# A decode kernel: TensorE's program shortened with loops, output turns moved ahead of w2, and hints on the last branches

## The chip, the cores and the metric

The kernel runs on one core of one Trainium2 chip. The metric is the device time of one execution in microseconds (us). Most numbers below are medians of five or six executions; the profile of a kernel is one execution with the profiler on. Kernels are compared only within the same rounds.

## The reference

It is one decoding step of a transformer block for 8 sequences: attention over a cache of 4096 keys, and an MLP beside it, both on the normalized input.

```python
# B, D = 8, 576; H, Sk, Dh = 32, 4096, 128; F = 4608; all bfloat16
x  = A_x
xn = _layernorm(x)
q  = (xn @ wq)                       # 8 x 32 heads x 128
p  = softmax(q . k_cache * Dh**-0.5) # k_cache, v_cache: 8 x 32 x 4096 x 128
o  = (p . v_cache) @ wo
y  = _layernorm(xn)
h  = gelu(y @ w1 + b1)
return x + o + (h @ w2 + b2)
```

The two caches are 537 MB. Everything else that is loaded (wq, w1, w2, wo) is 20 MB.

## The kernel before

The work is cut into 32 tiles of (sequence, 8 heads). K and V of a tile are 8.4 MB each and go through a ring of nearly three tiles in SBUF. SyncE issues all big DMAs in one order: wq, w1, K0, V0, K1, V1, ..., K31, V31, w2, wo. A tile's K is multiplied by the query on VectorE, summed on TensorE (with identity weights) and VectorE; V is multiplied on TensorE.

Before the first tile there is a head: layernorms, `turn_both` (small operands transposed on TensorE), `queries`, their broadcast, and the MLP's first layer with its gelu. V0 may not be loaded before the head's attention part is done, K1 not before the MLP part is done and the first two products of tile 0, V1 not before tile 0 has used V0:

```python
    def turn_both(e):
        for c in range(WC):                      # 9 matmuls
            i = e.matmul(tp[:, c], lhsT=dupv[:, c, :], rhs=two, start=True, stop=True)
        return i
    # ... cut ...
    def queries(e):
        for c in range(WC):                      # 36 matmuls, each into one of 4 groups of 32 columns
            wv = wq_sb[:, c, :].rearrange("p (x m d) -> p m x d", m=M, d=Dh)
            for m in range(M):
                i = e.matmul(
                    S_ps[0][m * MP:(m + 1) * MP, :], lhsT=xT[:, c, :], rhs=wv[:, m],
                    start=(c == 0), stop=(c == WC - 1))
        return i
    # ... cut ...
    for token in (wq_read, *head_done):
        od.wait("sync", token)
    load_kv(v_v, 0, 1)
    for token in mlp_done:
        od.wait("sync", token)
    for t in range(1, NT):
        sy.wait_ge(sem["kf"], NX * (t - 1) + 2)
        load_kv(k_v, t, 0)
        sy.wait_ge(sem["vf"], t)
        load_kv(v_v, t, 1)
```

After the last tile comes the tail: w2 (72 matmuls in two halves), the turning of the attention outputs (8 small matmuls) between the halves, and wo (64 matmuls in four pieces as they land):

```python
    CUTS = (0, 12, 23, 30, RO)                   # wo in pieces of 12, 11, 7, 2 rows; RO = 32
    # ... cut ...
    te.wait_ge(w2_in, 16)
    hidden_part()                                # 36 matmuls
    te.wait_ge(sem["on"], NT)
    ot = S_ps[0][:, :RO * B].rearrange("p (r b) -> p r b", b=B)
    for b in range(B):
        ins = te.matmul(
            ot[:, :, b], lhsT=Ox[:, b * NHG:(b + 1) * NHG].rearrange("p n g m -> p (n g m)"),
            rhs=low[:], start=True, stop=True)
    ins.then_inc(sem["end"], 1)
    hidden_part()                                # 36 matmuls
    te.wait_ge(sem["on"], NT + 1)
    for n, (r0, r1) in enumerate(zip(CUTS, CUTS[1:])):
        te.wait_ge(wo_in[n], 16)
        # ... two matmuls a row ...
    ins.then_inc(sem["end"], 1)
```

The softmax here doesn't subtract the row's maximum and nothing guards it: scores larger than these inputs give would overflow.

## Time and profile before

| | |
|---|---|
| time, first three executions | 1292.75 us (1292.69 to 1292.96) |
| span of the profiled execution (first to last instruction) | 1291.5 us |
| DMA rate over the span | 431 GB/s |
| busy: TensorE, VectorE | 57 %, 64 % |
| from one K or V tile's landing to the next | 19.35 us |

Parts of the page of the kernel before: the head line, and one line of the span in 40 equal slices. `DMA` is the busy share of the 16 DMA engines in tenths.

```profile
span 1291.5 us, 14658 instructions
...
DMA  9999999999999999999999999999999999999998
```

The DMA line is full up to the last slice. The view of waits says the same from the other side. Its columns are the waiting engine, its tile and line, whom it waited for, the total in us, how often, and the longest.

```profile
DVE ring L559 <- DMA ring<-in_A_k_cache_dram: 281.3, 31, 9.1
...
SPq L271 <- PE tot_ps L666: 634.8, 31, 20.7
SPq L271 <- PE s_ps L643: 525.7, 30, 17.6
```

VectorE waits up to 9 us in each tile for K, while SyncE waits for buffers with its queue still full. So the stream of DMA is the limit, and only three things can move the time: a gap in the stream, the last landing, and what comes after it. Two stretches must therefore be read closely. First, SyncE's issues in the head (start, duration, what):

```profile
1.26 0.33 SPq L271 DMA_DIRECT2D ring<-in_A_k_cache_dram  x1
23.95 0.33 SPq L271 DMA_DIRECT2D ring<-in_A_v_cache_dram  x1
53.53 0.33 SPq L271 DMA_DIRECT2D ring<-in_A_k_cache_dram  x1
74.24 0.33 SPq L271 DMA_DIRECT2D ring<-in_A_v_cache_dram  x1
92.05 0.33 SPq L271 DMA_DIRECT2D ring<-in_A_k_cache_dram  x1
```

These are K0, V0, K1, V1, K2. Each transfer lands in 16 parts; the first part of K1 lands at 83.28 us and the last at 85.16, so V1, issued at 74.24, is in the queue some 9 us before the stream needs it. That is the slack of the head. Second, the tail, from the timeline of the kernel before:

```profile
1277.94 3.67 PE L374 MATMUL acc<-ring,hT_sb 128*8 128x288 bf16 x36 [2.77 <-DMA ring<-in_B_w_dram]
...
1281.55 0.41 PE L692 MATMUL s_ps<-low,Ox 128*128 128x32 bf16 x8
...
1281.88 2.37 PE L374 MATMUL acc<-ring,hT_sb 128*8 128x288 bf16 x36
...
1284.09 3.29 PE L374 MATMUL acc<-ring,OT 128*8 128x288 bf16 x46
...
1288.31 1.27 PE L374 MATMUL acc<-ring,OT 128*8 128x288 bf16 x18 [0.92 <-DMA ring<-in_A_wo_dram]
...
1289.62 0.45 DVE L604 CAST fin<-acc 8x288 bf16<-8x288 f32 x1 [7.20 <-PE acc L374]
```

The bracket is the idle time before the group and what ended it. TensorE waits for w2 (2.77 us), works through it, and waits again for wo. The first 36 matmuls of w2 took 0.10 us each (3.67 / 36), the second 36 took 0.066: the granted clock was 0.50 of full speed from 1277.2 to 1280.6 us and 1.0 after it. The end of the chain of waits confirms who is last:

```profile
1259.74 28.52 DMA ring<-in_A_wo_dram
1288.26 0.04 issue
1288.31 1.29 PE acc L374 x18
1289.60 0.02 issue
1289.62 0.45 DVE fin L604
```

The third wo piece landed at 1288.26 and the fourth at 1288.96 (the landings in the trace).

### The profile page before, as it was taken

What the parts mean: (1) busy time and instruction counts of PE and PEld (TensorE: products, weight loads), DVE (VectorE), ACT (ScalarE), POOL (GpSimd) and SP (SyncE); (2) the same over time, 40 slices, a digit from 0 to 9 for tenths busy, and PEclk for the clock granted to TensorE, in tenths of its full rate; (3) what the DMA queues carried; (4) which work ended last, traced back from release to release, by engine and by line L of the source; (5) the groups of instructions that cost most, each with busy time, mean ns of one, the idle gap of its engine ahead of it and who ended that gap; (6) DMA issues with size and microseconds to landing.
All of it is one profiled execution on the core that took longest, in us unless ns stands there. A gap on an engine that the chain in (4) does not pass through costs nothing. (4 is left out here: it accounts for less than half of the span.)

```text
span 1291.5 us, 14658 instructions
## 1 busy us (share of the span) xinstructions
PE 736.8 (57%) x4707; PEld 322.3 (25%) x4707; DVE 829.4 (64%) x740; ACT 56.8 (4%) x181; POOL 2.4 (0%) x12
## 2 busy tenths in 40 slices
PE   4654565554565554665554565554566554565557
PEld 1222232222222222222222232222222222222223
DVE  2655677655677655677655677655677655577654
ACT  2000000000000000000000000000000000000000
POOL 0000000000000000000000000000000000000000
PEclk8778887778887777887777887778887777888779
DMA  9999999999999999999999999999999999999998
GB/s 419 441 427 440 430 428 449 422 428 449 422 428 449 422 430 447 422 436 440 424 436 438 426 438 434 428 442 428 428 449 422 428 449 422 428 449 422 430 447 350
DMA packets 10410, 557.02 MB, mean 431 GB/s; under 512 B 1163, under 2 KB 1188, under 8 KB 1446
## 3 DMA queue, kind: packets, MB, share of 16 engines
q1 hardware_dynamic: 10368, 556.93, 99.7%
q8 instruction: 3, 0.05, 0.0%
q10 hardware_dynamic: 38, 0.02, 0.0%
q14 instruction: 1, 0.01, 0.0%
HBM read 556.94 MB, written 0.01 MB: 431 GB/s over the span
## 5 line engine op out<-in xcount | busy, mean ns | idle before, releaser
L643 PE MATMUL s_ps<-ring,ident 128*128 x2048 | 544.5, 423 | 514.1 <-PEq L641 513.1
L559 DVE TENSOR_TENSOR ring<-ring,qb 128x4096 bf16<-128x4096 bf16 x256 | 579.2, 2283 | 281.6 <-DMA ring<-in_A_k_cache_dram 281.3
L643 PEld LDWEIGHTS s_ps<-ring,ident 128*128 128x128 bf16 x2048 | 217.4, 106 | 828.3 <-issue 678.5
L534 DVE TENSOR_REDUCE sc<-s_ps 128x32 f32<-128x512 f32 x256 | 171.8, 684 | 0.0
L662 PE MATMUL o_ps<-ring,ebd 128*32 128x512 bf16 x2048 | 116.4, 380 | 0.0
L546 DVE TENSOR_TENSOR ebd<-es,head 128x1536 bf16<-128x1536 bf16 x64 | 77.9, 1218 | 0.0
L569 DVE RECIPROCAL rec<-tot_ps 128x8 f32<-128x8 f32 x32 | 6.6, 208 | 110.7 <-PE oT_ps L670 110.7
L582 ACT ACTIVATE es<-sc 128x192 bf16<-128x192 f32 x64 | 19.8, 310 | 1104.2 <-DVE sc L534 1104.2
L662 PEld LDWEIGHTS o_ps<-ring,ebd 128*32 128x32 bf16 x2048 | 51.6, 97 | 62.5 <-issue 13.6
L670 PE MATMUL oT_ps<-selc,ob 128*128 128x8 f32 x256 | 33.9, 259 | 12.3 <-ACT ob L586 12.3
L670 PEld LDWEIGHTS oT_ps<-selc,ob 128*128 128x128 f32 x256 | 31.0, 191 | 15.2 <-ACT ob L586 15.2
L586 ACT ACTIVATE ob<-o_ps 128x512 f32<-128x512 f32 x32 | 19.1, 597 | 80.2 <-PE o_ps L662 80.2
L425 DVE TENSOR_SCALAR ring<-ring 96x384 f32<-96x384 f32 x2 | 0.7, 352 | 26.4 <-ACT ring L424 26.4
L545 DVE TENSOR_TENSOR Es<-Ep 128x1 f32<-128x1 f32 x32 | 5.1, 160 | 13.3 <-ACT es L582 13.3
L666 PEld LDWEIGHTS tot_ps<-headf,Es 128*128 128x128 f32 x64 | 9.5, 187 | 13.6 <-issue 13.6
L666 PE MATMUL tot_ps<-headf,Es 128*128 128x8 f32 x64 | 12.4, 266 | 0.0
L582 ACT ACTIVATION_READ_ACCUMULATOR es<-sc 128x1 f32 x64 | 11.9, 186 | 0.0
L414 PE MATMUL o_ps<-ring 128*32 128x384 bf16 x27 | 7.8, 860 | 2.8 <-DMA ring<-in_B_w_dram 2.8
L574 DVE TENSOR_TENSOR Ox<-on,quad 128x32 bf16 x32 | 6.2, 192 | 4.8
L414 PE MATMUL s_ps<-ring 128*32 128x384 bf16 x27 | 7.9, 862 | 0.0
L374 PE MATMUL acc<-ring,hT_sb 128*8 128x288 bf16 x72 | 6.0, 335 | 2.8 <-DMA ring<-in_B_w_dram 2.8
L336 PE MATMUL tot_ps<-ident,ring 40*128 40x16 bf16 x9 | 0.7, 204 | 11.8 <-DVE ring L314 11.8
(76 smaller groups left out, 61.2 us busy)
## 6 DMA issues: line engine op xcount, KB each, us to landing
ring<-in_B_w_dram SPq DMA_DIRECT2D x2, 5184.0 KB, 25.2
ring<-in_A_wq_dram SPq DMA_DIRECT2D x1, 4608.0 KB, 13.7
ring<-in_A_wo_dram SPq DMA_DIRECT2D x1, 1728.0 KB, 28.6
ring<-in_A_wo_dram SPq DMA_DIRECT2D x1, 1584.0 KB, 26.5
ring<-in_A_wo_dram SPq DMA_DIRECT2D x1, 1008.0 KB, 28.5
ring<-in_A_k_cache_dram SPq DMA_DIRECT2D x32, 31.9
ring<-in_A_v_cache_dram SPq DMA_DIRECT2D x32, 30.5
ring<-in_A_wo_dram SPq DMA_DIRECT2D x1, 288.0 KB, 28.8
```

Of the source, the lines that this page charges most:

```text
L414: i = e.matmul(h_ps[j][s * MP:(s + 1) * MP], lhsT=lhsT, rhs=wv[:, r0:r0 + HK, :], **flags)
L534: ins = ve.tensor_reduce(out=sc[:, n * CB:(n + 1) * CB], in_=bank_of(x).rearrange("p (c d) -> p c d", d=DL), axis=AX.X, op=ALU.add)
L546: ve.tensor_tensor(out=ebd[:, ja:jb], in0=es[:, a:b].rearrange("p (j c) -> p j c", c=4).unsqueeze(2) .to_broadcast([P, nj, G, 4]), in1=hea ...
L559: ve.tensor_tensor(out=k, in0=k, in1=qb[:, bass.ds(t, 1), :].to_broadcast([P, CB, Dh]), op=ALU.mult,).then_inc(sem["prod"], 1)
L569: ve.reciprocal(out=rec[:], in_=tot_ps[:, :G]).then_inc(sem["rec"], 1)
L574: ve.tensor_tensor(out=Ox[:, bass.ds(t, 1)].rearrange("p o g m -> p (o g) m"), in0=on[:].unsqueeze(2).to_broadcast([P, G, M]), in1=quad[:] ...
L582: sa.activation(out=es[:, a * CB:b * CB], in_=sc[:, a * CB:b * CB], func=ACT.Exp, scale=scale, accum_out=Ep[:, i:i + 1]).then_inc(sem["x"], 1)
L586: sa.activation(out=ob[:].rearrange("r c d -> r (c d)"), in_=o_ps, func=ACT.Copy).then_inc(sem["ob"], 1)
L643: ins = te.matmul(to, lhsT=idn, rhs=k[:, :, d * DL:(d + 1) * DL], start=(d == 0), stop=(d == Dh // DL - 1))
L662: ins = te.matmul(o_ps[m * MP:(m + 1) * MP, :], lhsT=ebd[:, j].rearrange("p g c -> p (g c)"), rhs=vals[:, c:c + 4, :], start=(j < M), stop ...
L666: te.matmul(tot_ps[:, :G], lhsT=Es[:].to_broadcast([P, P]), rhs=headf[:], start=True, stop=True).then_inc(sem["vf"], 1)
L670: ins = te.matmul(oT_ps[:, :G], lhsT=ob[:, c, :], rhs=selc[:, c, :], start=(c == 0), stop=(c == 3))
```

## The change

Its intent, as far as the diff shows it: a shorter TensorE program (about 705 instructions instead of about 790, as the prediction counts them), so that fewer blocks of instructions have to be fetched; small operands' turns and the queries become loops; the MLP layer works in groups of 512 columns; the output turns go ahead of w2, into TensorE's wait for it; and the last branch of VectorE and of TensorE gets a branch hint. Two small moves (a drain at the start, a buffer in the head) are left out below. The core of the diff:

```diff
+    def looped(name, n, **steps):
+        regs = {k: nc.alloc_registers(f"{name}_{k}", engines=[ENG.PE]) for k in steps}
+        # ... registers set, jump to a block of its own; close() adds the steps and branches back ...
     def turn_both(e):
-        for c in range(WC):
-            i = e.matmul(tp[:, c], lhsT=dupv[:, c, :], rhs=two, start=True, stop=True)
-        return i
+        (c, at), close = looped("turn_both", WC, c=(0, 1), at=(0, 2 * B))
+        e.matmul(
+            tot_ps[:, bass.ds(at, 2 * B)], lhsT=dupv[:, bass.ds(c, 2 * D - WC + 1)][:, ::WC],
+            rhs=two, start=True, stop=True)
+        close()
+        return nothing(e, oT_ps[:1, :1], idn[:, :1], idn, True)
     def queries(e):
-        for c in range(WC):
-            ... four matmuls, each into its own 32 columns ...
+        def part(at, w, start):
+            wv = ring[:, bass.ds(w, HQ)].rearrange("p (x m d) -> p m x d", m=M, d=Dh)
             for m in range(M):
+                e.matmul(
+                    S_ps[0], lhsT=xTz[:, bass.ds(at + (M - 1 - m) * MP, P)], rhs=wv[:, m],
+                    start=start and m == 0, stop=False)
+        part(0, 0, True)
+        (at, w), close = looped("queries", WC - 1, at=(M * MP, M * MP), w=(HQ, HQ))
+        part(at, w, False)
+        close()
+        return nothing(e, S_ps[0][:, :1], idn, xTz)
@@ layer @@
-        for j in range(HJ):
-            for s in range(HS):
-                ... 2 x 3 matmuls of 384 columns ...
+        for j, s, r0, r1 in HG:      # 4 matmuls of 512 columns, 1 of 256
+            i = e.matmul(h_ps[j][s * MP:(s + 1) * MP], lhsT=lhsT, rhs=wv[:, r0:r1, :], **flags)
@@ tail @@
+    vector_last = nc.mark_branch_hint_location(ENG.DVE)      # at VectorE's start
+    ve.br("vector_end").branch_hint(vector_last)             # at its end
+    place = nc.mark_branch_hint_location(ENG.PE)             # after the last tile
+    te.wait_ge(sem["on"], NT)
+    heads = Ox[:].rearrange("p t g m -> p (t g m)")
+    (b, at), close = looped("turn_out", B, b=(0, 1), at=(0, P))
+    te.matmul(
+        S_ps[0][:, bass.ds(b, RO * B - B + 1)][:, ::B], lhsT=heads[:, bass.ds(at, P)], rhs=low[:],
+        start=True, stop=True)
+    close()
+    nothing(te, S_ps[1][:1, :1], idn[:, :1], idn, True).then_inc(sem["end"], 1)
     te.wait_ge(w2_in, 16)
     hidden_part()
-    te.wait_ge(sem["on"], NT)
-    ... the 8 output turns, written out ...
     hidden_part()
     # ... wo as before ...
+    te.br("tensor_end").branch_hint(place)
```

(`nothing` is a matmul of one column whose end is signalled; a loop has no last matmul that could carry the signal.)

## The prediction

> **What bounds it now.** The DMA stream. The page's slices show DMA at 9 tenths or more in all but the last slice, 431 GB/s mean. Each 8.4 MB K or V tile lands 19.35 us after the one before (trace landings). The engines wait: the view of waits has VectorE 281 us on K tiles, the SP queue over 1100 us on buffers. So only what delays the stream, the last landing, or the work after it, can move the time. The chain of waits ends: last wo pieces landed 1288.26 and 1288.96 us, 18 matmuls (1.27 us), VectorE copy 0.45 us, output DMA 1.4 us.

> **What changes.**
> 1. Fewer TensorE instructions (about 790 to 705, from the build): of the three TensorE fetches (29.9, 76.0, 1287.1 us) I expect one, near 50 us. The VectorE hint should suppress the one at 52 us. The tail depends on the latest engine, so going from three late engines to one gains only 0.1 to 0.2 us. None late would gain 1.3 us.
> 2. Head: the looped turn costs about 0.5 us a pass (register ops 0.12 each, compare-branch 0.27, read off the product loop): 9 passes, 4.5 us for 0.7. Queries lose the four concurrent column groups (36 matmuls of 512 columns in 4.0 us): alone 0.427 us each at the cold clock, half warm: about 10 us, ending near 27 us instead of 17.9. Layer: same column total, about 13.7 us. VectorE's first tile starts at 52 to 54 us instead of 46.8. It is absorbed: V1 is issued at 74.2 us while K1 streams until 83, so 7 to 9 us are free.
> 3. Tail: the eight output turns (0.41 us) become a loop of about 4 us from 1276, ahead of w2, which landed at 1277.9. The w2 part then starts near 1280, with more of it at the 0.5 clock (0.102 us a matmul cold, 0.066 warm). Before, TensorE waited about 1.3 us for wo; that is used up: matmuls end near 1290.3 instead of 1289.6. This costs 0 to 1.5 us.
> [...]

> Sum: -0.15 + 0.8 - 0.2, about +0.4 us.

> **Predicted: 1293.1 us, range 1291.3 to 1294.8.** Faster by over 2%: 0.005; within 2%: 0.97; slower by over 2%: 0.025.

> **Signs.** Right: landings still 19.35 us apart; TensorE fetch packets 3 to 1; queries 10 us; V1 issued before 83 us; no TensorE wait on wo in the tail. Wrong: a gap in the DMA slices before 100 us; all three late DMA engines gone and the last landing near 1287.6 (then near 1291.5 us); an out-turn loop much under 4 us.

> **What would make it wrong by much.** The build puts a block boundary inside the TensorE product loop, run 256 times. [...] VectorE's loop of before seems to span a boundary with a single fetch, so I give this little chance.

Its sum came to about +0.4 us with all its terms; the -0.2 in it is the term of the end hints, worked out from no measurement. Without that term the sum is +0.65. A block is, here and below, what one fetch packet of 16384 bytes brings; where blocks end in the program is the author's reading of the build.

## The result and the profile after

| | before | after |
|---|---|---|
| time, six executions each | 1292.82 us (1292.69 to 1293.05) | 1294.51 us (1294.10 to 1295.43) |
| span of the profiled execution | 1291.5 us | 1293.4 us |
| its time less its span (unrounded, 1291.52 and 1293.38) | 1.36 us | 1.36 us |
| last wo landing | 1288.96 us | 1289.11 us |
| VectorE's copy of the result starts | 1289.62 us | 1291.47 us |
| last output transfer is issued | 1290.09 us | 1291.94 us |

The ratio is 1.0014, with a 95 % interval of 1.0001 to 1.0027. A ratio here is the mean time of one kernel's fast runs over that of the other's in the same rounds, so not quite the ratio of the medians above. Within 2 % it is the same; it is slower by 1.7 us all the same, and none of the six runs overlaps a run of before. The profiled executions differ by 1.86 us in time and by 1.85 us in the start of the final copy. So all of the loss arises before that copy, and nothing is gained or lost behind it.

The same two lines of the kernel after. The DMA line is as full as it was, up to the last slice:

```profile
span 1293.4 us, 14753 instructions
...
DMA  9999999999999999999999999999999999999997
```

SyncE's issues in the head, K0 to K2:

```profile
1.26 0.33 SPq L288 DMA_DIRECT2D ring<-in_A_k_cache_dram  x1
33.48 0.33 SPq L288 DMA_DIRECT2D ring<-in_A_v_cache_dram  x1
59.76 0.33 SPq L288 DMA_DIRECT2D ring<-in_A_k_cache_dram  x1
80.46 0.33 SPq L288 DMA_DIRECT2D ring<-in_A_v_cache_dram  x1
91.52 0.33 SPq L288 DMA_DIRECT2D ring<-in_A_k_cache_dram  x1
```

V0 is 9.5 us later, K1 and V1 6.2 us, K2 not at all. V1, at 80.46 us, is still ahead of K1's first landing (83.16). The cause is in the head's groups of the kernel after (busy us, mean ns of one, then idle before and why):

```profile
L409 PE MATMUL s_ps<-ring 128*128 (+1 forms) x36 | 10.7, 473 | 0.5 <-DVE ring L384 0.5
L375 PE MATMUL tot_ps<-ident,ring 40*128 40x16 bf16 x9 | 2.0, 221 | 14.5 <-DVE ring L331 12.0 <-issue 2.5
```

The same group of queries took 4.0 us before (36 matmuls of 512 columns), four column groups side by side; now a matmul starts 0.427 us after the one before it until 22.6 us. The nine turns now last from 11.99 to 16.46 us in the timeline; before they took 0.70 us. K1 lands at 85.01 us (85.16 before), V1 at 104.36 (104.51): the later head left no gap.

The tail of the kernel after, from its timeline (the first and last pass of the loop are shown):

```profile
1276.16 0.23 PE L738 MATMUL s_ps<-low,Ox 128*128 128x32 bf16 x1 [1.14 <-DVE Ox L619]
...
1280.00 0.23 PE L738 MATMUL s_ps<-low,Ox 128*128 128x32 bf16 x1 [0.29 <-issue]
...
1280.26 7.24 PE L421 MATMUL acc<-ring,hT_sb 128*8 128x288 bf16 x72
...
1287.33 4.09 PE L421 MATMUL acc<-ring,OT 128*8 128x288 bf16 x64
1291.47 0.45 DVE L649 CAST fin<-acc 8x288 bf16<-8x288 f32 x1 [10.58 <-PE acc L421]
```

No TensorE group after the loop has an idle time in brackets: TensorE no longer waits for wo at all. The end of the chain of waits, in which DMA no longer appears:

```profile
1280.00 0.23 PE s_ps L738
1280.24 0.02 issue
1280.26 0.16 PE s_ps L366
1280.42 11.02 PE acc L421 x135
1291.44 0.02 issue
1291.47 0.45 DVE fin L649
```

The 1.85 us can be added up from the two timelines. The w2 matmuls start 2.32 us later (1277.94 to 1280.26). From their start to the first wo matmul it is 6.15 us before, with the turns in the middle, and 7.07 us after, without them: 0.92 more. From there to the copy it is 5.53 us before, with the waits for wo, and 4.14 after, without: 1.39 less. 2.32 + 0.92 - 1.39 = 1.85. The middle term depends on where the half clock ended in these two executions.

The loop goes round every 0.53 us, of which a matmul shows 0.23 busy. And the clock is still down when w2 starts. In stretches of the kernel after, from 1276.00 to 1280.40 and from there to the end of w2 (busy time of each engine and instruction counts, then granted clock, DMA share, GB/s):

```profile
1276.00:1280.40 4.40, 2.01 (x11) 0.96 (x13) 0.00 (x0) 0.00 (x0) 0.00 (x0) 0.50 1.01 427
1280.40:1287.30 6.90, 6.90 (x73) 4.31 (x70) 0.42 (x1) 0.00 (x0) 0.00 (x0) 0.61 0.94 391
```

The clock's own records put the half clock from 1275.49 to 1285.73 us, three stretches of 3.413 us, against one such stretch (1277.22 to 1280.64) before. So 5.5 us of the w2 part ran at half clock, against 2.7 before. That is not the loop's doing alone: in head_last_hint below, without the loop, TensorE waits idle for w2 and 6.0 us of the w2 part run at half clock. In both records every stretch of either clock is 3.413 us or a multiple of it (up to seven times), but for the last, which the end of the record cuts short. What decides between the two clocks the records do not say, and TensorE's busy time as profiled gives no sharp limit: at half clock, a stretch of 3.41 us with 2.70 busy (24 matmuls, 1277.22 to 1280.64) was followed by the full clock in the kernel before, and one with 2.76 busy (22 matmuls, 1278.90 to 1282.32) by more half clock in the changed kernel.

### The profile page after: what moved, and what is told of

The parts are those of the page before. It is cut to its first block, busy times and chain, and to the rows that moved or that the text cites. A ratio compares the mean times of both kernels' runs of the same rounds, so it can differ in the third digit from the quotient of the medians.

```text
span 1293.4 us, 14753 instructions
## 1 busy us (share of the span) xinstructions
PE 739.4 (57%) x4700; PEld 325.1 (25%) x4700; DVE 829.5 (64%) x740; ACT 56.5 (4%) x181; POOL 3.2 (0%) x12
## 5 line engine op out<-in xcount | busy, mean ns | idle before, releaser
L690 PE MATMUL s_ps<-ring,ident 128*128 x2048 | 537.1, 418 | 514.9 <-PEq L688 514.9
L460 PE MATMUL o_ps<-ring 128*32 128x512 bf16 (+1 forms) x40 | 12.8, 1079 | 0.0
L627 ACT ACTIVATION_READ_ACCUMULATOR es<-sc 128x1 f32 x64 | 11.9, 186 | 0.0
L409 PE MATMUL s_ps<-ring 128*128 (+1 forms) x36 | 10.7, 473 | 0.5 <-DVE ring L384 0.5
```

The source lines that it names most:

```text
L409: e.matmul(S_ps[0], lhsT=xTz[:, bass.ds(at + (M - 1 - m) * MP, P)], rhs=wv[:, m], start=start and m == 0, stop=False)
L460: i = e.matmul(h_ps[j][s * MP:(s + 1) * MP], lhsT=lhsT, rhs=wv[:, r0:r1, :], **flags)
L627: sa.activation(out=es[:, a * CB:b * CB], in_=sc[:, a * CB:b * CB], func=ACT.Exp, scale=scale, accum_out=Ep[:, i:i + 1]).then_inc(sem["x"], 1)
L690: ins = te.matmul(to, lhsT=idn, rhs=k[:, :, d * DL:(d + 1) * DL], start=(d == 0), stop=(d == Dh // DL - 1))
```

## The experiments

Two theories were tested. The *loop theory*: the loss is TensorE's tail, that is the loop's 4 us in front of w2 and the half clock at which w2 then runs. The *fetch theory*: the loss is on the DMA side, from instruction fetches among the last transfers (the after trace has one at 1284.0 us), and from the head. A further question is what the fetches do to the stream at all. "Before" beside each run is the kernel before in the same rounds.

| run | time us (range) | before in the same rounds |
|---|---|---|
| turn_flat | 1293.19 (1292.77 to 1293.38) | 1292.92 (1292.81 to 1293.41) |
| before_turn_loop | 1294.18 (1293.83 to 1294.61) | the same |
| no_hints | 1294.17 (1293.94 to 1294.95) | the same |
| turn_loop_warm | 1293.12 (1292.86 to 1294.10) | the same |
| tail_of_before | 1292.92 (1292.90 to 1293.49) | 1292.88 (1292.68 to 1293.23) |
| head_last_hint (one look) | 1292.88 | the same |
| head_last_pad (one look) | 1293.08 | the same |
| before_cuts | 1293.04 (1292.93 to 1293.18) | 1292.94 (1292.83 to 1293.09) |
| flat_cuts | 1293.21 (1292.91 to 1293.86) | the same |
| before_warm_cuts | 1293.11 (1292.95 to 1293.57) | 1293.03 (1292.71 to 1293.23) |
| flat_warm_cuts | 1293.02 (1292.98 to 1294.20) | the same |
| short_loop (one look, other work) | 1293.75 | 1292.95 |

The intervals of the ratios of all these runs include 1 (they are some 0.13 % wide to either side), so the statements below rest on the medians, on ranges that do or do not overlap, and on what the profiles show. Two upper ends are no matter of the kernel's work: the executions of 1293.86 us (flat_cuts) and 1294.20 us (flat_warm_cuts) have spans of 1291.4 and 1291.7 us, so they lost about 1 us outside the span.

### turn_flat: the loop undone, its new place kept

```diff
-    (b, at), close = looped("turn_out", B, b=(0, 1), at=(0, P))
-    te.matmul(S_ps[0][:, bass.ds(b, ...)][:, ::B], lhsT=heads[:, bass.ds(at, P)], rhs=low[:], ...)
-    close()
-    nothing(te, S_ps[1][:1, :1], idn[:, :1], idn, True).then_inc(sem["end"], 1)
+    for b in range(B):
+        ins = te.matmul(ot[:, :, b], lhsT=Ox[:, b * NHG:(b + 1) * NHG]..., rhs=low[:], ...)
+    ins.then_inc(sem["end"], 1)
```

> The changed kernel with the eight output turns written out again instead of looped, still ahead of w2. Loop theory (the loss is TensorE's tail: a 4 us loop in front of the w2 matmuls, with the clock left at half): the w2 matmuls start at their landing near 1277.9, TensorE waits for wo again, last matmul near 1289.6 instead of 1291.4, time 1292.6 to 1293.0, as before. Rival (fetch theory: the loss is on the DMA side, from the instruction fetch at 1284 us that lands among the wo transfers, and from the later head): time stays near 1294.5.

Measured: 1293.19 us. Its range lies wholly under that of the changed kernel. That kernel was not run again in these rounds; no_hints, which differs from it in the hints alone, was, and its range lies wholly above too. From the timeline of this run:

```profile
1276.23 0.41 PE L738 MATMUL s_ps<-low,Ox 128*128 128x32 bf16 x8 [0.84 <-DVE Ox L619]
1278.15 6.25 PE L421 MATMUL acc<-ring,hT_sb 128*8 128x288 bf16 x72 [1.52 <-DMA ring<-in_B_w_dram]
...
1288.49 1.27 PE L421 MATMUL acc<-ring,OT 128*8 128x288 bf16 x18 [0.91 <-DMA ring<-in_A_wo_dram]
```

The turns take 0.41 us and end before w2 lands, and TensorE waits for w2 and wo again. An instruction fetch among the last transfers is still there (at 1280.1 us), and the last landing is at 1289.15. So the loop theory holds and the fetch theory doesn't. It comes 0.2 us above the top of what was expected; its profiled execution has K and V landing 0.2 us later than before (V31 complete at 1265.77 against 1265.54), which accounts for it there.

### before_turn_loop: the looped turns alone, in the kernel before

```diff
-    te.wait_ge(w2_in, 16)
-    hidden_part()
     te.wait_ge(sem["on"], NT)
-    ... 8 turns written out ...
+    ... the loop of the changed kernel ...
+    te.wait_ge(w2_in, 16)
+    hidden_part()
     hidden_part()
```

> The kernel before with one part of the change alone: the looped output turns ahead of w2. Loop theory: 1294.2 to 1294.8, the whole loss, with the head, the fetches at 30, 52 and 76 us unchanged. Fetch theory: 1292.8, no loss.

Measured: 1294.18 us against 1292.92, and the ranges do not overlap. With the head and the fetches of before (29.9, 51.6 and 75.7 us), this part alone brings 1.3 us, as much as all of the change without its hints in the same rounds (no_hints, 1294.17). In its timeline the loop runs from 1276.14 to 1280.0, w2 from 1280.05, and wo follows with no wait:

```profile
1280.05 6.88 PE L398 MATMUL acc<-ring,hT_sb 128*8 128x288 bf16 x72
1286.76 4.09 PE L398 MATMUL acc<-ring,OT 128*8 128x288 bf16 x64
```

### no_hints: both hints taken away

```diff
-    vector_last = nc.mark_branch_hint_location(ENG.DVE)
-    ve.br("vector_end").branch_hint(vector_last)
-    block("vector_end", ENG.DVE)
-    place = nc.mark_branch_hint_location(ENG.PE)
-    te.br("tensor_end").branch_hint(place)
-    block("tensor_end")
```

> The changed kernel without its two end hints and the end blocks they name. Loop theory: time unchanged within 0.3 us of the changed kernel (about 1294.5). The VectorE fetch packet at 52 us should come back; if the hints are worth anything at the end, the difference of time and span (1.36 us) grows. Fetch theory: a change of the time by up to 1 us, as fetches in the tail move.

Measured: 1294.17 us, in the range of the changed kernel. The time is 1.37 us over the span, against 1.36 with the hints, so at the end they are worth nothing that can be seen. What they do is visible only among the fetch packets: the VectorE packet is back (at 57.1 us), and the TensorE packet at 1291.1 us, with which the changed kernel ends, is gone. The one at 1283.9 stays. Both hints went at once, but head_last_pad and short_loop keep VectorE's alone, and there too no packet of the second kind falls into the stream. So VectorE's hint takes its fetch out of the stream, and TensorE's takes none out. Whether the packet at 1291.1 is the hint's is not shown: turn_flat has the hint and no such packet.

### turn_loop_warm: the loop kept, TensorE kept busy in it

```diff
     te.matmul(S_ps[0][:, bass.ds(b, ...)][:, ::B], lhsT=heads[:, bass.ds(at, P)], rhs=low[:], ...)
+    te.matmul(o_ps, lhsT=idn, rhs=qb[:, :NB // Dh, :], start=True, stop=True)
     close()
```

> The changed kernel with one idle 128x512 matmul into a free bank in each pass of the output-turn loop, so that TensorE is busy from 1276 to 1280 and its clock may rise before the w2 matmuls. Loop theory with the clock as half of it: w2 matmuls take about 4.8 to 5.5 us instead of 6.9, last matmul near 1289.6 to 1290.3, time 1292.8 to 1293.6. If the clock does not matter, or the granted clock does not answer: 1294.5 or a little more.

Measured: 1293.12 us, with the loop as long as ever. The same two stretches of this run, the loop and the w2 part:

```profile
1276.00:1280.60 4.60, 4.07 (x18) 1.04 (x20) 0.08 (x1) 0.00 (x0) 0.00 (x0) 0.63 0.99 421
1280.60:1285.20 4.60, 4.60 (x78) 3.91 (x79) 0.42 (x1) 0.00 (x0) 0.00 (x0) 1.00 1.01 428
```

Busy for 4.07 of 4.60 us instead of 2.01 of 4.40, TensorE is granted the full clock from 1279.8 us on. The w2 part takes 4.4 us (1280.59 to 1285.00) instead of 7.1, and a wait for wo comes back:

```profile
1288.42 1.27 PE L421 MATMUL acc<-ring,OT 128*8 128x288 bf16 x18 [0.41 <-DMA ring<-in_A_wo_dram]
```

One of its five executions, at 1294.10 us with a span of 1292.7, is as slow as the plain loop; it has no kept trace, so why is open.

The other half, no loop but a long half clock, is in the trace of head_last_hint (below, with the turns written out ahead of w2; one look). Its half clock lasts until 1283.96, as long as in no_hints (1284.13):

```profile
1277.96 7.50 PE L421 MATMUL acc<-ring,hT_sb 128*8 128x288 bf16 x72 [1.47 <-DMA ring<-in_B_w_dram]
1285.29 4.27 PE L421 MATMUL acc<-ring,OT 128*8 128x288 bf16 x64
```

The w2 part takes 7.3 us, even longer than in the changed kernel, but it starts at its landing. TensorE is through the first two wo pieces about when the third lands (1288.25), and the copy starts at 1289.60, as before. So the loop's length and the half clock are both needed for the loss: with either taken away TensorE is done with w2 and the first wo pieces by the time the third wo piece lands. The three profiles with the plain loop also suggest why its times are scattered (1.3 us between the fastest and the slowest of six, 0.4 us before). The half clock ends at a different time in each execution:

```text
                   half clock ends   copy of the result starts   time of that execution
no_hints               1284.13             1290.67                   1293.94
before_turn_loop       1284.78             1290.89                   1294.18
changed kernel         1285.73             1291.47                   1294.74
```

These are three kernels, one execution each. They rank as the theory says; that the end of the half clock causes the whole scatter is likely but not shown.

### tail_of_before: the head and the hints alone

```diff
+    te.wait_ge(w2_in, 16)
+    hidden_part()
     te.wait_ge(sem["on"], NT)
-    ... the loop ...
-    te.wait_ge(w2_in, 16)
-    hidden_part()
+    ... 8 turns written out ...
     hidden_part()
```

> The changed kernel with the tail of before (first half of w2, output turns written out, second half of w2), so the head's part of the change and the hints alone. Loop theory: V1 issued near 80.5 us, before its 83 us deadline, so the slower head costs nothing: 1292.7 to 1293.2, equal to the run with written-out turns ahead of w2. Rival (a part of the loss is the head's): 1293.5 or more.

Measured: 1292.92 us against 1292.88. V1 is issued at 79.25 us. The slower head costs nothing, and the written-out turns ahead of w2 (turn_flat) bring nothing over their old place either.

### The fetches in the stream: head_last_hint, head_last_pad, short_loop

The trace has 16 landings for every big DMA. The prediction takes each for the part of one of the core's 16 DMA engines; the traces show the parts, not whose they are, so it is parts that are counted below. Fetches are the packets that the profile calls "instruction" (1.0 to 1.2 us for 16384 bytes in the two kernels' traces). The page does not name their engines; the runs do: the packets of 16384 bytes move when TensorE's program is laid out anew (29.9 and 76.0 us before, 39.6 after, 5.9 and 11.6 in head_last_hint), and the one of 8192 bytes goes and comes back with VectorE's hint. TensorE itself lost nothing by the fetch at 39.6 us: in the timeline its matmuls show no idle time from 35.4 to 46.6 us. These are landings of V31, with each part's time after the first part, and the fetch packets that came before it (T: TensorE's queue, 16384 bytes; V: the other one, 8192 bytes), taken from the trace:

```text
before      T 29.9, V 52.2, T 76.0   0.00 0.01 0.01 0.06 0.12 0.26 0.26 0.28 0.33 0.38 0.44 0.45 0.49 1.66 1.73 1.84   complete 1265.54
after       T 39.6                   0.00 0.13 0.15 0.20 0.27 0.28 0.33 0.41 0.52 0.62 0.66 0.67 0.74 0.87 1.17 1.76   complete 1265.39
head_last_hint  T 5.9, T 11.6        0.00 0.01 0.03 0.07 0.08 0.16 0.19 0.19 0.21 0.22 0.27 0.36 0.37 0.50 1.44 1.70   complete 1265.57
short_loop  none                     0.00 0.01 0.12 0.17 0.21 0.30 0.33 0.34 0.38 0.39 0.40 0.41 0.42 0.51 0.53 0.56   complete 1264.28
```

The head_last runs lay TensorE's start-up code behind the rest of its program (with the turns written out), so that it is fetched at its first jump and not in the stream:

```diff
-    block("head")
-    ... start-up code ...
-    te.br("tile")
     block("tile")
     # ... tile loop, tail ...
     te.br("tensor_end")
+    block("head")
+    head_start = nc.mark_branch_hint_location(ENG.PE)
+    ... start-up code ...
+    te.br("tile").branch_hint(head_start)
     block("tensor_end")
```

> The changed kernel with the output turns written out, the TensorE start-up code laid out behind the rest of its program (so that it crosses a 16 KB block boundary in its first instructions, not in the middle), and the TensorE hint put on the jump from there to the tile loop instead of the end. Fetch-lag theory (an instruction fetch during the stream sets one DMA engine back by about 1.2 us for good, and the last landing waits for the latest engine): if no fetch packet of a TensorE or VectorE queue falls between 2 and 1280 us, the 16 parts of a K landing stay within 0.5 to 0.9 us and the last wo lands near 1287.9 to 1288.1 instead of 1289.1, time 1291.5 to 1292.0. With one fetch left in the stream: one late part, 1292.7 to 1293.2. Rival (the late parts have another cause): three or so late parts whatever the fetches do.

Measured: 1292.88 us in one look. The fetches moved to 5.9 and 11.6 us, still in the stream, because the first data were already moving at 1.04 us. The first jump took 6.9 us (1.36 to 8.25 us in the trace), and the packet at 5.9 us falls into it. Here that costs nothing: TensorE's first matmul waits for VectorE until 11.9 us (before: 11.8). What tells is that two late parts are there from the very first landing (wq: 1.70 and 1.93 us after its first part), where the kernel before has none (0.73 at most), its fetches coming later. The hint on TensorE suppressed nothing.

> As the one before, without its TensorE hint, but with 24 instructions that are never executed in front of the start-up code, so that all of it lies within one block and its boundary is crossed at the first jump, before the stream starts. Fetch-lag theory: as above, 1291.5 to 1292.0 if no fetch falls into the stream, else one late part for each that does. Rival: late parts stay.

Measured: 1293.08 us in one look. The padding was removed when the program was built, as code that is never reached, so this is the same layout without the hint: fetches at 6.1 and 11.8, two late parts from the first landing on (two more slide to about 1.0 us by the end). It only shows that the hint made no difference.

short_loop gives wrong outputs, for the same DMA traffic: enough matmuls are left out that TensorE's program up to the end of the tile loop fits into one block.

```diff
-        pe(["q", "sel"], [key], broadcast)
+        if b < 2:
+            pe(["q", "sel"], [key], broadcast)
-    for c in range(WC):
+    for c in range(1):                 # layer
         for j in range(a * J // NCB, b * J // NCB):
+            if j % 32 >= M:            # values
+                continue
-    ... TensorE's hint ...
```

> Wrong outputs on purpose, same DMA traffic: the changed kernel with written-out output turns, without the TensorE hint, and with most matmuls of the head's broadcasts and layer and of the values part left out, so that TensorE's program up to the end of the tile loop fits into its first 16 KB block and no instruction fetch should fall into the stream before about 1276 us. Fetch-lag theory: no late part in any landing (16 parts within 0.5 to 0.9 us), so the last V tile is complete at 1264.2 to 1264.7 instead of 1265.4 to 1265.7; a fetch near 1276 to 1280 then sets one engine back, so the time gains little: 1292.3 to 1293.1. Rival (late parts come from something else): late parts of 1.6 to 1.9 us stay, V complete near 1265.5.

Measured: no fetch before 1275.0 us, and no late part: all 16 within 0.56 us, V31 complete at 1264.28 us, 1.26 us earlier than in the kernel before. Then the fetch at 1275.04 comes, and every landing after it has exactly one late part (1.75 us in w2's). The last wo lands at 1288.86, and the copy starts at 1289.52. This is the clearest of the runs: one fetch packet, one part set back by some 1.2 us (1.75 in w2's landing, where the latest of V31's is at 0.56) in every landing after it, and the landing waits for it. The other traces agree step by step: in no_hints, for example, the first landing after the fetch at 39.7 us has one part over 1 us behind the first (1.95), and the first landing after the one at 57.1 us has two (1.84 and 1.95). (The time of this single run, 1293.75, is 0.8 us over that of before while its span is 1291.4; a fetch packet at 1292.8 us, after the span, goes with it. Its outputs were within the tolerance although most of the work was missing, so the comparison with the reference is not sensitive to it.)

It also shows why the changed kernel gained so little from its shorter program. With one late part the landing is nearly as late as with three: V31 at 1265.39 against 1265.54.

### Looking for a faster tail: before_cuts, flat_cuts, before_warm_cuts, flat_warm_cuts

```diff
-    CUTS = (0, 12, 23, 30, RO)
+    CUTS = (0, 12, 20, 26, 30, RO)
```

> The kernel before with wo loaded in five pieces (12, 8, 6, 4, 2 rows) instead of four (12, 11, 7, 2), nothing else. If the end of before hangs on the last landings and the matmuls that wait for them (18 matmuls in 1.27 us after 1288.26), then 12 matmuls remain after that landing and 4 after the last at 1288.96: last matmul near 1289.25 instead of 1289.58, time 0.2 to 0.4 us less, 1292.4 to 1292.7. If the end hangs on something else: no difference.

Measured: 1293.04 us against 1292.94: no gain. The profile says why, in its chain of waits:

```profile
1277.95 4.49 PE acc L374 x36
1282.43 0.54 PE s_ps L692 x8
1282.97 6.64 PE acc L374 x98
1289.62 0.02 issue
```

In this execution the half clock lasted until 1283.77, and the chain runs through TensorE without a wait for wo. So in the kernel before, too, TensorE and the landings arrive at nearly the same time, and the end of the half clock (1283.77 here, 1280.64 in the profile of before above) can decide which is last.

> The changed kernel with the output turns written out, ahead of w2, and the same five pieces of wo. As the run with written-out turns, less 0.2 to 0.4 us: 1292.5 to 1292.9, so no slower than the kernel before and perhaps a little faster. If it stays at 1293.0 or more, the shorter last piece is worth nothing.

Measured: 1293.21 us, above the expected range, so worth nothing here either.

The last two runs add idle matmuls that keep the clock up while TensorE waits for w2:

```diff
+    for _ in range(6):
+        te.matmul(o_ps, lhsT=idn, rhs=qb[:, :NB // Dh, :], start=True, stop=True)
     te.wait_ge(sem["on"], NT)
```

> The kernel before with five wo pieces, the output turns (written out) ahead of w2, and six idle 128x512 matmuls into a free bank between the last tile and those turns, to keep TensorE's clock up until w2 lands. If the tail is set by the later of two things, the landings (last at 1289.0) and TensorE's w2 and wo matmuls at whatever clock was granted, then with the clock up the w2 part takes about 4.8 us, TensorE waits for every wo piece, last matmul 0.3 to 0.45 us after the last landing: 1292.4 to 1292.7. If the clock is not kept up: 1292.9 to 1293.3 as without the idle matmuls.

> The same two additions on the changed kernel with written-out output turns: 1292.5 to 1292.8 if the clock stays up, so faster than the changed kernel by about 1.8 us and level with or a little below the kernel before; else 1293.0 to 1293.5.

Measured: 1293.11 and 1293.02 us against 1293.03. The clock did stay at 1.0, from 1254 us until after the last matmul, and w2 took 4.4 us. TensorE waited for every wo piece but the first, which had landed at 1281.97, before w2 was done. From before_warm_cuts:

```profile
1277.88 4.58 PE L374 MATMUL acc<-ring,hT_sb 128*8 128x288 bf16 x72 [1.24 <-DMA ring<-in_B_w_dram]
...
1288.35 1.11 PE L374 MATMUL acc<-ring,OT 128*8 128x288 bf16 x12 [0.53 <-DMA ring<-in_A_wo_dram]
...
1289.51 0.45 DVE L604 CAST fin<-acc 8x288 bf16<-8x288 f32 x1 [12.41 <-PE acc L374]
```

Yet the copy starts at 1289.51 instead of 1289.62: a tenth of a microsecond, which the times don't show. The landing at 1289.0 is the floor here. No version was found that beats the kernel before. By this reasoning the only one that might is a whole program without a fetch in the stream, and that was not to be had: it would have to do everything up to the end of the tile loop in the first block.

## Why the prediction was right, and where it was not

The time was within the range, and within 2 % as forecast, though near the upper end: two of the six executions (1295.03 and 1295.43) lie above it. The mechanisms that decide were right; the balance was mis-sized, +0.4 us predicted and +1.7 us measured.

- *The stream bounds the kernel, and the head's delay is absorbed.* Right. Queries took 10.7 us (about 10 predicted), VectorE's first product came at 53.05 us (52 to 54), V1 was issued at 80.46 us (before 83), and tail_of_before shows that the head costs nothing.
- *Tail: "This costs 0 to 1.5 us", entered as +0.8.* This is the mis-sized term. The copy starts 1.85 us later. The loop was foreseen (about 4 us, w2 near 1280; measured 1280.26), and so was the end of the waits for wo. What was underrated is the clock: the matmuls of w2 and the end near 1290.3 imply some 6.2 us for w2 (1290.3 less 1280 less the 4.1 us that the wo matmuls took), and it was 7.1, because 5.5 us of it ran at half clock. The prediction had said "more of it at the 0.5 clock", but gave it no time. How much more is partly luck: w2 took 6.3 us in no_hints and 6.7 in before_turn_loop, which have the same loop. turn_loop_warm shows that the clock matters: w2 in 4.4 us, and the loss is gone.
- *Fetches: "of the three TensorE fetches ... I expect one", -0.15.* Wrong in its count. There are three again, at 39.6, 1284.0 and 1291.1 us: one fewer in the bulk of the stream, but one among the wo transfers, so the last landing became 0.15 us later (1289.11) and not earlier. Until that fetch the forecast held: the first wo piece was complete at 1281.88 us, against 1282.04 before. It did not matter, as TensorE ended later still. The VectorE part was right: its packet at 52 us is gone, and no_hints brings it back. The underlying claim, that each fetch sets one part back by about 1.2 us and that the latest part alone counts, is borne out by short_loop: none late gave 1.26 us where 1.3 was said. That a part stands for one DMA engine, as the prediction has it, was not shown.
- *End hints: entered as -0.2.* Nothing was measured: time less span is 1.36 us before, 1.36 after and 1.37 without hints.
- *A block boundary in the product loop might cause fetches at every pass.* It did not: the trace has no fetch packet between 39.6 and 1284.0 us, that is none in the whole tile loop.

In sum: -0.15 + 0.8 - 0.2 should have been about 0 + 1.85 + 0.

Left open: why VectorE's hint suppresses a fetch and TensorE's does not; why one part of the changed kernel's landings slides to 1.17 us near 90 to 104 us without a fetch; how much of the scatter of the times the end of the half clock explains; and what a few executions lose outside their span.

## What to carry to other kernels

A loop around a few tiny matmuls was not free on TensorE: a pass took 0.53 us, with 0.23 of a matmul and some 0.33 of register operations and a branch in it, and so little work (2.01 us busy of 4.40) left the granted clock at 0.50 for the dense work that followed, as did idle waiting in head_last_hint (6.0 us of w2 at half clock). Where a kernel ends on a balance of landings and matmuls, put work into a wait only if it is over before the wait is; and judge a shorter program by the blocks that it still fetches, not by its instructions, because one fetch in the full stream cost nearly as much as three (V31 at 1265.39 us against 1265.54, and 1264.28 with none).
